# Attention and a SiLU layer on one core: new planner constants, an earlier V load, an earlier first product and another way of storing the last tiles

## The chip, the cores and the metric

The kernel runs on one core of one Trainium2 chip. The core has a matmul engine (TensorE, PE in the profile, with its weight loads as PEld), VectorE (DVE), ScalarE (ACT), GpSimd (POOL) and SyncE (SP). The metric is the device time of one execution in microseconds (us); lower is better. Transfers between HBM and the on-chip buffer are issued by POOL (all loads), SP and ACT (all stores).

## The reference

Inputs are q, k and v of 8 batches, 12 heads, 448 tokens and 64 values a head, and two weight matrices, 768 x 2048 (w_in) and 2048 x 768 (w_out), all float32. Per batch and head it computes softmax(q k^T / 8) v; the heads of a token are put side by side (3584 tokens x 768), and then comes

```python
h = x @ w_in
g = h * (1.0 / (1.0 + np.exp(-h)))
return (g @ w_out).astype(np.float32)
```

The output is 3584 x 768 float32.

## The kernel before, in words

**Work.** Everything is held in fp16 on chip; loads convert on the way. For a batch and a group of four heads (a unit; the first batch's units are cut in two halves of the tokens, so there are 27 units) the kernel transposes k and q on VectorE (lines 328, 338), computes scores in bursts of 8 or 16 matmuls into tiles `s` (line 357), takes exp on ScalarE into tiles `E` (line 394), and multiplies with ones (part 0, the sums) and with V (parts 1 and 2) into tiles `a` (lines 420, 436). VectorE turns the sums into reciprocals (`sT`, `inv`, `rdn`) and writes the scaled result to `xT` (line 493), already in the layout that the next product reads. V of the first batch lies in the buffer named `D` in the profile.

**First layer.** For batches 0 to 3, and for a part of batches 4 and 5, tiles `h` are x times w_in in groups of six matmuls (line 345). ScalarE takes tanh (line 521) and VectorE (1 + tanh) times h (line 559), which is the SiLU because x was halved. The other batches go in pairs: seven products on sums of halves in place of eight (tiles `f`, line 650, with copies and adds at 663 and 666), and SiLU on ScalarE (line 676). The results are in `G` and `X`.

**Second layer.** The first two tiles of 128 output tokens are plain products (tiles `o`, 16 matmuls for each half of the columns). All others go in quads, two token tiles by two column halves: seven products of eight matmuls each (tiles `p`, in the order 1, 5, 6, 2, 7, 3, 4, function `product`, queued by `queue_quad`). Products 1 and 2 share a bank: ScalarE must copy product 1 (line 768) before product 2 may add to it. Outputs leave by `take_out` (ScalarE copies the bank to a tile `ost`, line 771) or `add_out` (VectorE, line 780), and `store` issues four transfers of 32 rows for each (line 763), on SP, and for the last two quads on SP and ACT in turn.

**Order.** One stream of instructions per engine is written out by a planner in the kernel itself. The class `Order` holds for each engine the time when it is free, by constants at the head of the file: `SWITCH` for a change of the kind of tile on TensorE, `mm` and `act` for durations, `DMA_ROW`, `DMA_RATE`, `DMA_START`, `DMA_TAIL` for loads. At each step the main loop looks at the next score burst (`qk_at`), the next attention product (`av_at`) and a list `moe` of first- and second-layer work (`moe_ready`), and emits one that is ready by these times. Products are queued in parts of `PROD_AT` matmul positions; between two parts another piece of work may come in. `LATE` tells how long after the planned landing V of the first batch counts as there. Where the planner finds TensorE idle in the opening it fills with products of zeros (line 1530). Rings (`s_ring`, `m_ring`, `ost_ring` and others) stand for the buffers: two for scores, four banks for `h`, `a`, `o`, `p`, `f`, four for `ost`.

**Loads.** POOL issues all loads in one order, set by the calls of `plan_k`, `plan_q`, `plan_v`, `plan_w_in` and `plan_w_out`: k and q of the three head groups of the first batch, its V in four loads, three more q, half of w_in, and so on.

The readiness rule that the change touches is in `queue_quad`:

```python
elif m == 1 and qd > 1:
    made.append((pr_op.get((qd - 1, 6)), 9.0))
```

Product 1 of a quad may go only when product 6 of the quad before has been placed.

Of the kernel before, what the change touches and what calls it, by code (L numbers as in the profile page):

```python
# [13 lines left out]
ENG = mybir.EngineType  # L14


SWITCH = 0.094
PE_OUT = 0.20
HOP = 0.10
DMA_ROW = 0.022  # L20
DMA_RATE = 13570.0
DMA_START = 1.2
DMA_TAIL = 1.0

# [1 line left out]
def mm(n):  # L26
    return n / 2400.0 + 0.0026


def act(n):  # L30
    return n * 0.00087 + 0.13
# [47 lines left out]
class Order:  # L79
# [33 lines left out]
    def on_pe(self, op, mode):  # L113
        if mode == "full" and self.attention:
            mode, op.strips = "cols", True
        gap = SWITCH if mode != self.mode else 0.0
        self.mode = mode
# [3 lines left out]
    def load(self, rows, row_bytes, emit, ring=None, gate=None):  # L121
        op = Op("POOL", 0.58, emit)
        self.pool.append((op, rows * (DMA_ROW + row_bytes / DMA_RATE) / 16, ring, gate))
        return op
# [50 lines left out]
def kernel(  # L175
# [9 lines left out]
    nc = tc.nc  # L185

    B, NH, S, D = q.shape
# [3 lines left out]
    NG = NH // HG  # L191
    TPP = S // 32
# [9 lines left out]
    NT = 2 * S // 128  # L202
    OH = DM // 2
# [3 lines left out]
    NPL = 4  # L207
    EAGER = 1
    HALVES = 6
    NEAR, LATE = 0.15, -2.0  # L210
    COLD, FIRST = 8.5, 47
    SHY = 0.6
    TWB, SXB, FAR = 2, 2, 8
# [50 lines left out]
    rawk, rawq, KT, QT, E, T, acc, rdn_t, xT, g_t, ost_t = ({} for _ in range(11))  # L264
# [101 lines left out]
    def per_burst(n):  # L366
        return 2 if units[n][0] == 0 else 1
# [315 lines left out]
    S_t, tmp_t, ost_t, pr_t = {}, {}, {}, {}  # L683
# [57 lines left out]
    def bank(qd, m):  # L741
        return pr_t[(qd, m)][:, 0:OH]
# [5 lines left out]
    def ost(qd, i, j):  # L748
        t = sb.tile([128, OH], FP32, name=f"ost_{qd}_{i}{j}", tag="ost", bufs=NOST)
        ost_t[(qd, i, j)] = t  # L750
        return t

    def store(qd, i, j):
        u, t = divmod(2 * qd + i, NT)
        for w in range(4):
            r, col = divmod(128 * t + 32 * w, S)
            b = 2 * u + r
            dst = out[b * S : (b + 1) * S, OH * j : OH * (j + 1)].rearrange(
                "(i g) m -> g i m", g=TPP
            )  # L760

            eng = nc.scalar if w % 2 and 4 * qd + 8 >= NT * B else nc.sync
            eng.dma_start(  # L763
                out=dst[col // 32], in_=ost_t[(qd, i, j)][32 * w : 32 * (w + 1), :]
            )

    def take(qd, m):
        nc.scalar.copy(out=tmp(qd, m), in_=bank(qd, m))

    def take_out(qd, m, i, j):  # L770
        nc.scalar.copy(out=ost(qd, i, j), in_=bank(qd, m))  # L771
        store(qd, i, j)

    def add_in(qd, to, x, y):
# [25 lines left out]
    def plan_k(b, hg):  # L800
        ld_k[(b, hg)] = od.load(128, 2 * D * TPP, lambda: load_k(b, hg), rk_ring)

    def plan_q(n):
        g0, g1 = units[n][2:]
        ld_q[n] = od.load(128, 2 * D * (g1 - g0), lambda: load_q(n), rq_ring)

    def plan_v(b, hg0, hg1):
        made = []
        for x in range(4):
            ring = v_ring if (x == 0 and b > 0) else None  # L810
            heads, toks = HG * (hg1 - hg0), X_TOK[form(b, hg0)][x][1]
            made.append(
                od.load(32 * heads, 2 * D * toks, lambda x=x: load_v(b, hg0, hg1, x), ring)
            )
        for hg in range(hg0, hg1):
            ld_v[(b, hg)] = made
# [12 lines left out]

    NB0 = NG * len(PIECES)  # L830
    for hg in range(NG):
        plan_k(0, hg)
        plan_q(hg)
    plan_v(0, 0, NG)
    plan_q(NG)
    plan_q(NG + 1)
    plan_w_in(0, DFF // 2)
# [14 lines left out]
    for n in range(NB0 + NG, NU):  # L852
        b, hg = units[n][:2]
# [34 lines left out]
    pr_op, sg_op, w_op, plain_op = {}, {}, {1: [], 2: [], 3: []}, {}  # L888
    inv_op, norm_op = [], []
    quads, fourth, begun = [], [], []  # L890

    PROD_AT, FFN1_AT = 2, 2

    def in_parts(n, size, columns, emit, done, at=0):
        to = min(at + size, n)
# [311 lines left out]
    def queue_quad(qd):  # L1207
        quads.append(qd)
        fourth.append(qd)
        took = {}  # L1210

        def read(name, eng, fn, deps, then=None):
            busy = act(OH) if eng == "ACT" else OH / 960.0 + 0.13
            bias = -2 if eng == "ACT" else -4
            took[name] = od.add(Op(eng, busy, fn, deps, bias, then=then))

        def out(at):
            m_ring.give(at)
            ost_ring.give(at + STORE)

        def queue(m):
            def run():
                if BANK[m] == m:
                    m_ring.take()
                for ring, need in rings:
                    ring.take(need)
                in_parts(HF, PROD_AT, OH, lambda f0, f1: product(qd, m, f0, f1), done)

            def done(op):
                if m == 5:  # L1230
                    sg_ring.give(od.free["PE"] + PE_OUT)
                pr_op[(qd, m)] = op
                if m in (1, 5):
                    read(m, "ACT", lambda: take(qd, m), [op])
                elif m == 6:
                    read("u", "DVE", lambda: add_in(qd, 6, 6, 1), [op, took[1]], tmp_ring.give)
                    read("w", "DVE", lambda: add_in(qd, 5, 6, 5), [took["u"], took[5]])
                elif m == 2:
                    read("11", "ACT", lambda: take_out(qd, 1, 0, 0), [op], out)
                elif m == 7:  # L1240
                    read(
                        "22",
                        "DVE",
                        lambda: add_out(qd, 6, 5, 1, 1),
                        [op],
                        lambda at: (ost_ring.give(at + STORE), tmp_ring.give(at)),
                    )
                elif m == 3:
                    read("12", "ACT", lambda: take_out(qd, 5, 0, 1), [op], out)
                else:  # L1250
                    read("21", "ACT", lambda: take_out(qd, 6, 1, 0), [op], out)

            def deps():
                made = list(w_op.get(m, [None]))
                made += [took.get(x) for x in {2: (1,), 7: ("w",), 3: ("w",), 4: ("22",)}.get(m, ())]
                first = {5: 1, 6: 5, 7: 6, 3: 7, 4: 3}.get(m)
                if first:
                    made.append((pr_op.get((qd, first)), 9.0))
                elif m == 1 and qd > 1:
                    made.append((pr_op.get((qd - 1, 6)), 9.0))  # L1260
                if m in (1, 2, 4):
                    t = 2 * qd + (m == 4)
                    for b in {(128 * t + c) // S for c in (0, 127)}:
                        for f in range(HF):
                            x = g_op.get((b, f + HF * (m > 1)), [None])
                            made += [(y, f * mm(OH)) for y in x]
                    return made + ld_wout
                x = sg_op.get((qd, {5: 1, 6: 2, 7: 3, 3: 4}[m]), [])
                x = x if len(x) == 2 else [None, None]
                return made + [x[0], (x[1], 4 * mm(OH))]  # L1270

            rings = ((tmp_ring, 1),) if m in (1, 5) else ((ost_ring, 1),) * (m != 6)
            moe.append((deps, int(BANK[m] == m), run, rings))

        for m in (1, 5, 6, 2, 7, 3, 4):
            queue(m)
# [86 lines left out]
    def run_qk():  # L1363
        ns, c, ys = qk_seq.pop(0)
        n = ns[0]
        nq = 32 * (units[n][3] - units[n][2])
        s_ring.take(len(ys))
        if ys[0] == 0:
            e_ring.take()
        rest = len(ns) == 2  # L1370
        op = Op(
            "PE",
            2 * per_burst(n) * mm(nq) + (0.03 if rest else 0.013),
            (lambda: scores_rest(n)) if rest else (lambda: scores(n, c, ys)),
            tail=PE_OUT,
        )
        op.half = len(ys) == 1
        if c == NCH // per_burst(n) - 1 and ys[-1] == 1:
            done = []
            for m in ns:  # L1380
                if last_unit[units[m][:2]] == m:
                    done.append(kt_ring)
                done.append(rq_ring)
            op.then = lambda at: [r.give(at) for r in done]
        od.on_pe(op, "rest rows" if rest else "rows")
        for y in ys:
            made = od.add(
                Op(
                    "ACT",
                    act(2 * nq * per_burst(n)),  # L1390
                    lambda y=y: expo(n, c, y),
                    [op],
                    tail=0.2,
                    then=s_ring.give,
                )
            )
            for m in ns:
                exp_op.setdefault(m, []).append(made)
        if form(*units[n][:2]) != "lone" and c == 1 and ys[-1] == 1:
            adds.append(n)  # L1400
# [134 lines left out]
    while True:  # L1535
# [48 lines left out]
        if warm["on"] and od.free["PE"] <= od.now and wait > 0.06 and od.now > 0.9:  # L1584
            each = mm(128) if od.now > COLD else 0.107
            n = max(1, int((wait - 0.06) / each), int(wait / each + 0.9) * (od.now < COLD))
            if warm.pop("first", None):
                n = FIRST
# [36 lines left out]
```

## Time and profile before

| what | us |
|---|---|
| median of 3 runs | 393.24 (393.09 to 393.57) |
| the profiled execution's own time | 392.73 |
| its span, first to last instruction | 391.0 |
| TensorE busy | 383.1 |
| VectorE busy | 275.0 |
| ScalarE busy | 257.7 |
| granted TensorE clock, mean | 0.999 |

The span is what lies between the first and the last instruction in the profile; the rest of the execution's own time lies around it. Busy times are sums per engine, and an engine that is not on the chain of work that ended last may be idle at no cost. Times of events are counted from the start of the span.

### The profile page before, as it was taken

Reading aid. Unit: us, or ns where it says so; the run is one execution under the profiler, and the core shown is the slowest. Engines: PE = TensorE matmul, PEld = TensorE weight load, DVE = VectorE, ACT = ScalarE, POOL = GpSimd, SP = SyncE. Lnnn points to the kernel's source line nnn. Section 1 sums busy time; section 2 is a strip of 40 time slices with the busy share of each in tenths; the row PEclk is TensorE's granted clock in tenths of the full one; section 3 lists DMA queues with packets and bytes.
Section 4 is the critical chain, followed back from the end, with each engine's and each line's share of the span. In section 5 each row is a group of like instructions: output and inputs, shape, how many; then the busy total and the mean of one; then the engine's idle time right before and its main releaser. Section 6 shows DMA issues by size and latency. Waiting matters only on the chain.

```text
span 391.0 us, 13258 instructions
## 1 busy us (share of the span) xinstructions
PE 383.1 (98%) x5662; PEld 208.8 (53%) x5662; DVE 275.0 (70%) x571; ACT 257.7 (66%) x424; POOL 83.7 (21%) x153
## 2 busy tenths in 40 slices
PE   8999999999999999999999999999999999999995
PEld 6668764444445444455544454455546654555663
DVE  3476676999997858896878998599876235547322
ACT  4988885697967686966688776746763246763221
POOL 7532543604160422415060500000000000000000
PEclk9999999999999999999999999999999999999999
DMA  7999999834584672829492522210001330001343
GB/s 117 207 209 209 166 182 184 144 65 58 85 123 82 104 138 32 115 45 150 109 142 36 73 47 64 57 29 1 2 0 43 100 100 3 1 2 31 98 108 89
DMA packets 35594, 34.68 MB, mean 89 GB/s; under 512 B 11600, under 2 KB 34000, under 8 KB 35536
## 3 DMA queue, kind: packets, MB, share of 16 engines
q0 software_dynamic: 24784, 22.82, 39.0%
q1 hardware_dynamic: 9984, 10.24, 10.0%
q10 hardware_dynamic: 768, 0.79, 0.8%
q8 instruction: 44, 0.72, 0.8%
q14 instruction: 14, 0.11, 0.1%
HBM read 45.61 MB, written 11.01 MB: 145 GB/s over the span
## 4 chain that ended last, share of the span: by engine, by line
PE 94%; ACT 2%; DVE 2%; DMA 1%; issue 1%; ACTq 0%; DVEq 0%; POOLq 0%
PE p L345 30%; PE h L345 23%; PE s L357 13%; PE f L650 13%; PE a L420 11%; PE o L345 3%; PE a L436 2%; DMA rk<-in_k_dram 1%; ACT E L394 1%; DVE f L666 1%; PE z L1530 1%; ACTq L763 0%; DVE p L775 0%; ACT G L676 0%; ACT ost L771 0%
## 5 line engine op out<-in xcount | busy, mean ns | idle before, releaser
L394 ACT ACTIVATE E<-s 128x896 f16<-128x896 f32 (+1 forms) x172 | 151.2, 916 | 50.6 <-PE s L357 49.3
L345 PE MATMUL h<-xT,w_in_t 128*32 128x448 f16 (+2 forms) x1542 | 94.4, 342 | 0.0
L345 PEld LDWEIGHTS <-w_in_t 128*32 128x32 f16 (+1 forms) x1542 | 53.5, 97 | 38.2 <-issue 12.6
L345 PEld LDWEIGHTS <-G 128*32 128x32 f16 (+1 forms) x1184 | 52.6, 97 | 39.0 <-issue 8.4
L345 PE MATMUL p<-w_out_t,G 128*32 128x384 f16 (+1 forms) x872 | 66.2, 327 | 0.2
L293 POOL DMA_DIRECT2D V<-in_v_dram x84 | 46.0, 559 | 60.0 <-PE a L420 46.5
L357 PE MATMUL s<-rq,KT 32*128 32x448 f16 (+4 forms) x864 | 56.9, 340 | 1.2 <-ACT E L394 0.8
L559 DVE SCALAR_TENSOR_TENSOR G<-th,h 128x448 f16<-128x448 f16 (+2 forms) x92 | 44.3, 498 | 13.2 <-ACT th L521 13.1
L521 ACT ACTIVATE th<-h 128x448 f16<-128x448 f32 (+1 forms) x92 | 42.2, 485 | 16.8 <-PE h L345 9.8
L771 ACT COPY ost<-p 128x384 f32<-128x384 f32 x39 | 18.7, 481 | 33.2 <-PE p L345 24.1
L345 PE MATMUL p<-D,S 128*32 128x384 f16 (+1 forms) x496 | 37.4, 327 | 0.0
L420 PE MATMUL a<-E,V 128*32 128x448 f16 (+1 forms) x672 | 36.3, 353 | 0.0
L493 DVE SCALAR_TENSOR_TENSOR xT<-a,rdn 128x448 f16<-128x448 f32 (+1 forms) x54 | 30.1, 568 | 8.3 <-PE a L420 6.4
L357 PEld LDWEIGHTS <-KT 32*128 32x128 f16 (+2 forms) x864 | 17.6, 98 | 29.6 <-issue 27.2
L676 ACT ACTIVATE G<-f 128x448 f16<-128x448 f32 (+1 forms) x52 | 25.9, 529 | 10.6 <-PE f L650 6.8
L279 POOL DMA_DIRECT2D rq<-in_q_dram x27 | 15.0, 556 | 73.5 <-PE s L357 51.6
L345 PEld LDWEIGHTS <-S 128*32 128x32 f16 (+1 forms) x496 | 20.6, 97 | 14.5 <-issue 2.3
L666 DVE TENSOR_TENSOR f<-f,q 128x448 f32<-128x448 f32 x26 | 16.4, 632 | 15.6 <-PE f L650 14.2
L405 DVE TENSOR_TENSOR T<-T,E 128x1792 f16<-128x1792 f16 x20 | 21.7, 1085 | 7.8 <-ACT E L394 7.8
L420 PEld LDWEIGHTS <-V 128*32 128x32 f16 (+1 forms) x672 | 17.1, 96 | 16.4 <-issue 5.8
L405 DVE TENSOR_TENSOR T<-E,E 128x1792 f16<-128x1792 f16 x20 | 21.7, 1084 | 4.4 <-ACT E L394 4.3
L650 PEld LDWEIGHTS <-w_in_t 128*128 128x128 f16 x156 | 15.3, 98 | 14.1
(135 smaller groups left out, 384.8 us busy)
## 6 DMA issues: line engine op xcount, KB each, us to landing
out_dram<-ost SPq DMA_DIRECT2D x208, 48.0 KB, 1.6
rk<-in_k_dram POOLq DMA_DIRECT2D x24, 224.0 KB, 5.2
rq<-in_q_dram POOLq DMA_DIRECT2D x21, 224.0 KB, 4.9
w_in_t<-in_moe_w_in_dram POOLq DMA_DIRECT2D x6, 512.0 KB, 11.2
w_out_t<-in_moe_w_out_dram POOLq DMA_DIRECT2D x4, 768.0 KB, 13.2
V<-in_v_dram POOLq DMA_DIRECT2D x43, 64.0 KB, 4.0
V<-in_v_dram POOLq DMA_DIRECT2D x40, 48.0 KB, 3.7
out_dram<-ost ACTq DMA_DIRECT2D x16, 48.0 KB, 1.8
```

The source lines that it names most:

```text
L293: nc.gpsimd.dma_start(out=v_of(b, hg0)[32 * x : 32 * (x + 1), at, 0:count, :], in_=v[b, hs].rearrange("h (i g) d -> i h g d", g=TPP)[:, :, ...
L345: nc.tensor.matmul(out=out[at], lhsT=lhsT[:, at], rhs=rhs, **flags)
L357: nc.tensor.matmul(out=pS[p0 : p0 + 32 * (x1 - x0), h % 2, at : at + nq], lhsT=KT[(b, hg)][32 * h : 32 * (h + 1), c, x0:x1, :, e], rhs=QT[ ...
L394: nc.scalar.activation(out=E[(n, w)][0:kr, 2 * y : 2 * y + 2, 0:nk], in_=pS_t[(n, w, y)][0:kr, :, 0:nk], func=AF.Exp, scale=attn_scale,)
L405: nc.vector.tensor_tensor(out=T[n], in0=T[n] if step else E[(n, 0)], in1=E[(n, step + 1)], op=ALU.add,)
L420: nc.tensor.matmul(out=a[32 * h : 32 * (h + 1), 0:nq], lhsT=w, rhs=e[k0:k1, h, at : at + nq], start=start, stop=stop,)
L493: nc.vector.scalar_tensor_tensor(out=x3(b, cc)[:, cc % 3, 32 * g0 : 32 * g1], in0=acc[(n, part)][:, 0:nq], scalar=0.5, in1=rdn_t[n].rearra ...
L521: nc.scalar.activation(out=th, in_=h_t[(b, f, t0)][:, 0 : t1 - t0], func=AF.Tanh)
L559: nc.vector.scalar_tensor_tensor(out=dst[:, f, at + lo : at + hi], in0=th_t[(b, f, t0)][:, lo - t0 : hi - t0], scalar=1.0, in1=h_t[(b, f, ...
L650: nc.tensor.matmul(out=pp_t[(f, PBANK[m])], lhsT=w[:, c, :], rhs=a[:, c, :], start=(c == 0 and m in (1, 6, 5)), stop=(c == 2), skip_group_ ...
L666: nc.vector.tensor_tensor(out=pp_t[(f, to)], in0=pp_t[(f, x)], in1=pf_t[(f, y)], op=ALU.add)
L676: nc.scalar.activation(out=dst[:, f, at + lo : at + hi], in_=pp_t[(f % HF, x)][:, lo:hi], func=AF.Silu, scale=2.0,)
```

## The change

Six things are changed together. The planner's constants for a change of tile kind, for loads, for score bursts and for exps have new values, and V of the first batch counts as there 1 us after its planned landing, not 2. V of the first batch is loaded after the third k and before the third q (the loop value 2 meets the second condition). Products of the second layer are queued matmul position by position, so a score burst may come between any two. Product 1 of a quad may go once product 1 of the quad before is placed. In the last quad the copy of the last product is VectorE's. And the four outputs of the last quad are stored by two transfers of 64 rows each, one from SP and one from ACT, in place of four of 32 rows.

```diff
-SWITCH = 0.094
+SWITCH = 0.104
 PE_OUT = 0.20
 HOP = 0.10
-DMA_ROW = 0.022
-DMA_RATE = 13570.0
+DMA_ROW = 0.012
+DMA_RATE = 14000.0
...
-    NEAR, LATE = 0.15, -2.0
+    NEAR, LATE = 0.15, -1.0
...
     def store(qd, i, j):
         u, t = divmod(2 * qd + i, NT)
+        if qd == NT * B // 4 - 1:
+            r, col = divmod(128 * t, S)
+            g, b = col // 32, 2 * u + r
+            dst = out[b * S : (b + 1) * S, OH * j : OH * (j + 1)].rearrange(
+                "(i g) m -> g i m", g=TPP
+            )
+            for w in range(2):
+                (nc.scalar if w else nc.sync).dma_start(
+                    out=dst[g + 2 * w : g + 2 * w + 2],
+                    in_=ost_t[(qd, i, j)][64 * w : 64 * (w + 1), :],
+                )
+            return
         for w in range(4):
...
     def take_out(qd, m, i, j):
-        nc.scalar.copy(out=ost(qd, i, j), in_=bank(qd, m))
+        if m == 6 and qd == NT * B // 4 - 1:
+            nc.vector.tensor_copy(out=ost(qd, i, j), in_=bank(qd, m))
+        else:
+            nc.scalar.copy(out=ost(qd, i, j), in_=bank(qd, m))
         store(qd, i, j)
...
     for hg in range(NG):
+        if hg == 2.5:
+            plan_v(0, 0, NG)
         plan_k(0, hg)
+        if hg + 0.5 == 2.5:
+            plan_v(0, 0, NG)
         plan_q(hg)
-    plan_v(0, 0, NG)
     plan_q(NG)
...
-    PROD_AT, FFN1_AT = 2, 2
+    PROD_AT, FFN1_AT = 1, 2
...
-                    read("21", "ACT", lambda: take_out(qd, 6, 1, 0), [op], out)
+                    eng = "DVE" if qd == NT * B // 4 - 1 else "ACT"
+                    read("21", eng, lambda: take_out(qd, 6, 1, 0), [op], out)
...
                 elif m == 1 and qd > 1:
-                    made.append((pr_op.get((qd - 1, 6)), 9.0))
+                    made.append((pr_op.get((qd - 1, 1)), 9.0))
...
-            2 * per_burst(n) * mm(nq) + (0.03 if rest else 0.013),
+            2 * per_burst(n) * mm(nq) + (0.041 if rest else 0.024),
...
-                    act(2 * nq * per_burst(n)),
+                    act(2 * nq * per_burst(n)) - 0.07,
                     lambda y=y: expo(n, c, y),
                     [op],
-                    tail=0.2,
+                    tail=0.27,
```

## The prediction

> **What bounds the kernel now.** I read the page's busy shares first, then the chain of work that ended last, then the timeline of TensorE (PE) for places where it pauses, and last the stores.
>
> ```profile
> span 391.0 us, 13258 instructions
> ...
> PE 383.1 (98%) x5662; PEld 208.8 (53%) x5662; DVE 275.0 (70%) x571; ACT 257.7 (66%) x424; POOL 83.7 (21%) x153
> ...
> q1 hardware_dynamic: 9984, 10.24, 10.0%
> q10 hardware_dynamic: 768, 0.79, 0.8%
> ...
> PE 94%; ACT 2%; DVE 2%; DMA 1%; issue 1%; ACTq 0%; DVEq 0%; POOLq 0%
> ...
> out_dram<-ost SPq DMA_DIRECT2D x208, 48.0 KB, 1.6
> ```
>
> PE is busy 98% and makes 94% of the chain: only a pause of PE, or work before its first and after its last product, can move the end. The timeline shows where these are (start, length, engine, line; idle time before it and what ended it in brackets):
>
> ```profile
> 12.88 0.57 PE L357 MATMUL s<-rq,KT 32*128 32x224 f16 x8
> ...
> 15.87 0.57 PE L420 MATMUL a<-E,D 128*32 128x224 f16 x16
> ...
> 60.27 0.55 POOL L279 DMA_DIRECT2D rq<-in_q_dram  x1 [3.67 <-DMA w_out_t<-in_moe_w_out_dram]
> ...
> 103.34 1.47 PE L345 MATMUL p<-w_out_t,G 128*32 128x384 f16 x32
> 104.74 0.60 PE L357 MATMUL s<-rq,KT 32*64 32x448 f16 x16
> 105.39 0.83 PE L345 MATMUL p<-w_out_t,G 128*32 128x384 f16 x16
> ...
> 166.11 1.48 PE L345 MATMUL p<-w_out_t,X 128*32 128x384 f16 x32 [0.61 <-ACT 1_3_4110 L768]
> ...
> 287.89 0.73 PE L650 MATMUL f<-xT,tw 128*128 128x448 f16 x3 [0.23 <-DVE f L666]
> ...
> 385.30 1.46 PE L345 MATMUL p<-D,G 128*128 128x384 f16 x8
> ...
> 387.24 0.48 ACT L771 COPY ost<-p 128x384 f32<-128x384 f32 x1 [0.99 <-DMA out_dram<-ost]
> 387.75 0.85 ACTq L763 DMA_DIRECT2D out_dram<-ost  x2
> ```
>
> Groups of matmuls that follow without a wait overlap by 0.16 in this record (1.46 shown for 1.30 of advance), so a pause is 0.16 more than the idle shown: 0.61 at 166.11 is 0.77. The last lines are the tail: the last product ends at 386.77, the last copy starts only at 387.24, since ACT was still issuing stores, and its four stores land until 389.97 by the landing marks; the span ends 1.03 later.
>
> The sum stands against this execution: span 391.0, its own time 392.73 (1.73 around the span). The median of the runs, 393.24, is 0.51 above it, and I add that at the end. 0.2% of it, 0.79 us, is about what a measurement of this kernel can tell from no change.
>
> **Part by part.**
>
> *Refitted constants, PROD_AT.* They change only the order. In the two built orders the same products stand (18 fills with zeros fewer), and PE changes its kind of tile between equally many stretches, 193 in each without the fills. A change costs 0.105 (a 448-column product's start to a score's start is 0.294 instead of 0.189). Equal counts: 0.
>
> *V ahead of the third q.* On POOL's queue the third q load is issued after four V loads (4 x 0.63), at 6.5 instead of 4.03. By the landing marks q landed at 10.38 and the last V at 14.42; the same bytes are ahead of whichever is last, so V lands at 13.6 to 14.2 and q at 13.8 to 14.4. PE now has the first product with V ahead of the third unit's scores. Counting by rows (0.50 a burst of scores or a product with its change), it reaches that product at 12.4 and waits 1.2 to 1.8; the scores start at 14.3 to 14.85 instead of 12.88. After that, 18 zero fills fewer (0.06 each and a change of kind) stand in the order and three first-layer groups (0.58 each) come earlier; at 32 us it is ahead by 0.2 to 0.75. Then it gives that back: the plain product of the first two output tiles takes its last quarter of w_out at 58.9 instead of 63.6, and the fourth w_out load landed at 59.7 (POOL's q load, held by it, starts at 60.27). It waits about 0.8, and from there the rows bring both orders to the same place near 75 us. All loads behind keep their places. Sum to 75: 0, bounds -0.3 and +0.3.
>
> *The first product early.* It may follow the previous quad's first product, so the copy (0.48 on ACT, behind exps of 0.92) has time before product 2 reads what it left. Where 0.75 and 0 us lay between products 1 and 2 (lines at 104.74 and 166.11), 4.5 to 5.1 lie in the new order; both waits go: -0.12 and -0.77. What is late next: the bank that product 1 holds longer; the shortest reuse distances of the four banks stay as they were (1.0 before, 0.9 after).
>
> *The pair stage, 269 to 293.* Four waits of 0.16, 0.39, 0.39 and 0.22 end by silu or add. One product moves under the third: 1.30 of cover instead of 1.13, -0.17. The waits at 323, 351 and 382 have the same neighbours and stay.
>
> *Waits that I can't see.* Before, 0.29 of small waits are left between 75 and 269. The new order is planned with an ACT 0.07 an exp faster and scores often 2.7 apart instead of 2.9. I take +0.3; bounds -0.3 and +1.2.
>
> PE's end: -0.12 - 0.77 - 0.17 + 0.3 = -0.76.
>
> *The last copy on VectorE.* No such copy is in the trace; nearest is the add on the same tile, 0.558 (L780), bounds 0.48 (ACT's copy) and 0.60. DVE is free, starts 0.03 after the product's end, at 386.81 instead of 387.24: ends 0.35 earlier.
>
> *64-row stores.* Eight instead of sixteen in the last quad, one issue less on each of SP's and ACT's queues: the last issue starts at once, not 0.42 later. A pattern of three dimensions may take longer to issue: between the 0.31 of these stores and the 0.72 of POOL's loads. Against that stands how a store is spread. 9984 packets for 208 stores are 48 each: 32 rows and 16 marks of 4 bytes, so a store of 32 by 384 lies on 16 engines, two rows on each. The new stores have 64 rows on the SBUF side but 2 x 32 on the other. No transfer of the trace from SP or ACT has such a count, so I bound it. One end: 16 engines, four rows each, two rows more at 0.09 (10.0% of 16 x 391 over 6656 rows) is +0.2; with copy and issue the tail is 0.6 shorter. Other end: the split runs along the outermost count and must fall in the same places on both sides. 64 and 2 then allow two pieces of 32 rows on two engines. Since both queues used the same 16 engines, all eight stores then fall on the same two: 4 x 64 = 256 rows each. A row takes 0.059 at the rate of the opening's k loads (8 rows of 3584 B an engine in 1.1 us) to 0.0895 (the mean packet above). I take 0.065, near the first, because a long queue resembles those loads. First issue 383.15 - 0.76, first packet 0.81 later (as the last stores show), + 16.6, mark to landing 0.36, to the end 1.03: 401.2, which is +10.2. DVE's early copy is buried under it, and PE isn't held: no output buffer of that quad is used again.
>
> Between these far ends I take the second: equal pieces of whole rows on each side is what all stores shown have, and with 2 there are only two.
>
> [...]
>
> Sum: 392.73 + 10.2 = 402.9; with the 0.51 of the median 403.4.
>
> **Rivals.**
>
> 1. *The stores spread over 16 engines* (not slower). Then -0.76 - 0.6: 392.73 - 1.4 + 0.51 = 391.9, bounds 390.9 and 393.1. For it: every store so far has 16 marks. Against: none has an outer count under 32. It decides at the split: over eight engines (32 rows each in all, about 2 us at 0.065, mostly beside the remaining products) it would still be no slower.
> 2. *Two engines a store, but others for each queue*: 128 rows, 8.3 us: 383.2 + 8.3 + 0.36 + 1.03 = 392.9, time 395.1. With a new pair for each store, 32 rows of 2.1 us behind the last copy end at 390.9: 393.1, no change. Against: both queues show the same 16 engines' marks.
> 3. *The early part takes the gain too*: the fourth w_out load lands 1 us later (they took 4.3, 3.6, 5.3, 4.2), or exps end late at the bursts 2.7 apart (0.1 at each of 30). Either takes rival 1's time to 393, within 0.2%.
> 4. *The freed waits come back* as a wait for a bank held by two first products: 0.9 more, 392.8 in rival 1.
>
> **How the numbers follow.** The same two engines: 0.55. Rival 1 as it stands 0.26, with rivals 3 or 4 in it 0.06 more. Rival 2: 0.13. The likeliest gives 403.4, its own range 401.5 (0.059 a row) to 409.7 (0.0895). Since 0.32 lies near 392, the range reaches down to rival 1: 391.0 to 408.5, which leaves out the slowest rows and rival 1's best edge. Faster: 0.26 less its part above 392.45, 0.24. Same: 0.10 from rivals 1, 3, 4 and the last of 2. Slower: 0.55 + 0.11, 0.66.
>
> **What the new profile would show.** The two hardware queues' last stores with long issue-to-landing times, several to 15 us, and DMA share near 2/16 with PE idle from 386: right. All landing within 2.2 us and the span under 390: rival 1. PE's last product should end near 386.0; no wait before any second product at 105 and 166; a wait before the w_out product near 59 us; a wait of 1.2 to 1.8 before the first product with V. The forecast falls with the split of the stores alone; if PE's end isn't 0 to 1.5 earlier, my reading of the order is wrong.

## The result, and the profile after

The changed kernel takes 411.76 us (median of 5, 411.05 to 413.04) against 393.11 of the kernel before on the same chip: 1.0472 times as long, 95% interval 1.045 to 1.0495. The forecast was 403.4, so the sign was right and the size 8.4 short. Against the span worked out there for the profiled execution, 401.2, it is 411.3.

The page after, in the order of the lines shown of before:

```profile
span 411.3 us, 13177 instructions
...
PE 390.2 (95%) x5626; PEld 211.2 (51%) x5626; DVE 276.2 (67%) x572; ACT 257.0 (63%) x423; POOL 83.6 (20%) x153
...
PEclk9856999999999999999999999999999999999995
...
q1 hardware_dynamic: 9864, 10.24, 9.5%
...
q10 hardware_dynamic: 648, 0.79, 0.7%
...
PE 89%; DMA 2%; DVE 2%; ACT 1%; POOL 1%; issue 1%; DVEq 0%; ACTq 0%; POOLq 0%
...
out_dram<-ost SPq DMA_DIRECT2D x200, 48.0 KB
```

PE is busy 7.1 us longer (390.2 against 383.1) although its real work is the same. The row `PEclk` is the granted clock in tenths of full speed, in 40 slices of the span; in the page of before it held only 9s:

```profile
PEclk9999999999999999999999999999999999999999
```

Now it has 8, 5 and 6 in its second to fourth slice, and a 5 in the last, where PE has nothing left to do. The packets of the two hardware queues give away how the new stores are split: 9864 is 200 stores of 48 and four of 66, 648 is eight of 48 and four of 66. A 64-row store is 64 rows and 2 marks, where a 32-row store was 32 rows and 16 marks.

The opening, in stretches of 3.41 us: in the traces of this case the time from one change of the recorded clock to the next is a multiple of 3.413 us (here 20.48 at half clock, 361.81 at full clock behind it). The columns are from, to and length; PE busy and its instructions; granted clock; DMA share; GB/s:

```profile
6.89:10.30 3.41, 2.96 (x44) 1.00 1.23 179
10.30:13.72 3.42, 3.04 (x63) 1.00 1.43 196
13.72:17.13 3.41, 1.60 (x41) 1.00 1.16 210
17.13:20.54 3.41, 3.41 (x53) 0.50 1.12 211
...
34.20:37.61 3.41, 3.41 (x46) 0.50 1.15 209
37.61:41.02 3.41, 3.33 (x88) 1.00 1.17 213
```

In one stretch PE was busy 1.60 of 3.41 us. At its end the clock falls to half, and it stays there for 20.5 us, six stretches, although PE is busy in all of them. The timeline shows what PE waited for:

```profile
13.37 0.57 PE L420 MATMUL a<-E,D 128*32 128x224 f16 x16 [0.38 <-DMA D<-in_v_dram]
...
15.28 0.78 DVE L338 STREAM_TRANSPOSE rq<-rq 128x224 f32<-128x224 f32 x2 [2.57 <-DMA rq<-in_q_dram]
...
15.75 0.57 PE L357 MATMUL s<-rq,KT 32*128 32x224 f16 x8 [1.81 <-DVE rq L338]
```

V was there at 13.33, earlier than forecast; the third q landed only at 15.26, behind it, and PE's next scores started when its transpose was done, at 15.75. The last product ended at 394.87 instead of 386.77.

The second loss follows that product. The copy on VectorE starts at 394.91, ends at 395.47, and its stores are issued 0.03 later. Then the core only waits for its stores (all engines; here PE, PEld, DVE, ACT, POOL busy, clock, DMA share of 16 engines, GB/s):

```profile
393.00:395.00 2.00, 1.87 (x12) 0.91 (x10) 0.09 (x1) 0.48 (x1) 0.00 (x0) 1.00 0.12 28
395.00:397.00 2.00, 0.00 (x0) 0.00 (x0) 0.47 (x1) 0.00 (x0) 0.00 (x0) 1.00 0.13 41
...
400.00:405.00 5.00, 0.00 (x0) 0.00 (x0) 0.00 (x0) 0.00 (x0) 0.00 (x0) 0.50 0.13 50
405.00:409.00 4.00, 0.00 (x0) 0.00 (x0) 0.00 (x0) 0.00 (x0) 0.00 (x0) 0.50 0.13 50
409.00:410.00 1.00, 0.00 (x0) 0.00 (x0) 0.00 (x0) 0.00 (x0) 0.00 (x0) 0.50 0.10 38
```

The last 4 us of the kernel before, whose last product ended at 386.77, in the same columns:

```profile
387.00:391.00 4.00, 0.00 (x0) 0.00 (x0) 0.00 (x0) 0.48 (x1) 0.00 (x0) 0.90 0.41 98
```

A share of 0.13 is two engines of sixteen, though both queues have stores waiting: they share the same two. From the last product's end to the span's end it is 16.4 us instead of 4.2.

So 20.3 us more span are 8.1 in PE's end and 12.2 behind it. Two of 68 executions of the kernel before were slow, with a mean clock of 0.956 and 0.953 (407.8 and 409.4 us), and so was one of four with the 128-row stores below (415.7 us, 0.948); these are left out of the ratios.

### The profile page after: what moved, and what is told of

The parts are those of the page before. It is cut to its first block, busy times and chain, and to the rows that moved or that the text cites. A ratio compares the mean times of both kernels' runs of the same rounds, so it can differ in the third digit from the quotient of the medians.

```text
span 411.3 us, 13177 instructions
## 1 busy us (share of the span) xinstructions
PE 390.2 (95%) x5626; PEld 211.2 (51%) x5626; DVE 276.2 (67%) x572; ACT 257.0 (63%) x423; POOL 83.6 (20%) x153
## 3 DMA queue, kind: packets, MB, share of 16 engines
q1 hardware_dynamic: 9864, 10.24, 9.5%
## 4 chain that ended last, share of the span: by engine, by line
PE 89%; DMA 2%; DVE 2%; ACT 1%; POOL 1%; issue 1%; DVEq 0%; ACTq 0%; POOLq 0%
PE p L345 28%; PE h L345 22%; PE f L650 12%; PE s L357 12%; PE a L420 11%; PE o L345 3%; DMA rq<-in_q_dram 2%; PE a L436 1%; ACT E L394 1%; DVE f L666 1%; POOL D L293 1%; POOL rk L273 0%; DVE p L790 0%; DVE T L405 0%; POOL rq L279 0%
## 5 line engine op out<-in xcount | busy, mean ns | idle before, releaser
L345 PE MATMUL h<-xT,w_in_t 128*32 128x448 f16 (+2 forms) x1524 | 96.5, 343 | 0.2 <-DVE G L559 0.2
L357 PE MATMUL s<-rq,KT 32*128 32x448 f16 (+4 forms) x864 | 60.3, 357 | 2.6 <-DVE rq L338 1.8
L493 DVE SCALAR_TENSOR_TENSOR xT<-a,rdn 128x448 f16<-128x448 f32 (+1 forms) x54 | 30.4, 569 | 11.9 <-PE a L420 10.1
L357 PEld LDWEIGHTS <-KT 32*128 32x128 f16 (+2 forms) x864 | 19.3, 105 | 33.6 <-issue 29.8
L345 PEld LDWEIGHTS <-S 128*32 128x32 f16 (+1 forms) x496 | 20.5, 97 | 14.9 <-issue 3.1
```

Source lines behind the costliest of these rows:

```text
L345: nc.tensor.matmul(out=out[at], lhsT=lhsT[:, at], rhs=rhs, **flags)
L357: nc.tensor.matmul(out=pS[p0 : p0 + 32 * (x1 - x0), h % 2, at : at + nq], lhsT=KT[(b, hg)][32 * h : 32 * (h + 1), c, x0:x1, :, e], rhs=QT[ ...
L493: nc.vector.scalar_tensor_tensor(out=x3(b, cc)[:, cc % 3, 32 * g0 : 32 * g1], in0=acc[(n, part)][:, 0:nq], scalar=0.5, in1=rdn_t[n].rearra ...
```

## The experiments

In most of them the part under test is the opening, so the mean clock of single executions is given: with 32-row stores 0.996 to 1.000 is a kept clock (what is missing lies behind the last product).

**The changed kernel with 32-row stores.** The branch of `store` for the last quad is taken out. The second run is the same kernel once more, to see how far the throttled stretch repeats.

```diff
     def store(qd, i, j):
         u, t = divmod(2 * qd + i, NT)
-        if qd == NT * B // 4 - 1:
-            ...
-            return
         for w in range(4):
```

> The changed kernel with its last quad stored in 32-row stores again (all else stays: V early, refitted constants, PROD_AT 1, last copy on VectorE). My theory is that two separate things cost the time: TensorE's clock, granted at 0.50 from 17 to 37 us, puts its last product at 394.9 instead of 386.8; and the 64-row stores add some 12 us behind that product. Then the last product still ends at 394 to 395, the mean clock stays at 0.96, and the span ends 3.9 behind it: about 400 us by the clock, 398 to 401 with the spread of the throttled time. If instead the late last product had to do with the stores (their issues stand in the queues of SP and ACT ahead of the last copies), the last product comes earlier than 392 and the time is below 396.

> A second copy of the previous kernel with one look, to see how far its last product and the length of the throttled stretch repeat: theory 394 to 395 and 17 to 20.5 us at 0.50.

Median 400.56 (397.53 to 403.36, four executions; mean clock 0.962 to 0.983), 1.0184 times before with a wide interval (1.0116 to 1.0251), and 401.4 (0.966) for the second. The share of the stores is gone, the other loss is there and even larger than I expected: the last product ends at 397.6 and at 395.6, and the half clock lasts nine and eight stretches. And the place was not the one that I expected. First the one, then the other run, in the same columns as above:

```profile
6.26:9.67 3.41, 1.80 (x34) 1.00 1.10 163
9.67:13.09 3.42, 3.42 (x31) 0.50 1.47 193
...
40.39:43.81 3.42, 3.33 (x88) 1.00 1.16 212
```

```profile
4.46:7.87 3.41, 2.48 (x49) 1.00 1.08 160
7.87:11.29 3.42, 2.87 (x50) 1.00 1.27 168
11.29:14.70 3.41, 3.41 (x51) 0.50 1.36 200
```

Here the clock fell at 9.67 and at 11.29, before PE came to the wait for the third q at all. In the first, q's first load landed at 6.96, where it had been 5.41 in the first profile of the changed kernel, and PE waited 1.26 us for it (1.18 in this stretch); in the second the stretch had only 0.55 us of waits. So the wait of 1.81 for the third q is one way to lose the clock, not the only one: three traces of this opening lost it in three places, and q's first load alone came 1.55 us later in one of them than in another.

**The kernel before with 64-row stores alone, and with 128-row stores.** The first adds the same branch of `store` to the kernel before; the second issues one store for each of the last four tiles:

```diff
+        if qd == NT * B // 4 - 1:
+            ...
+            (nc.scalar if j else nc.sync).dma_start(
+                out=dst[g : g + 4], in_=ost_t[(qd, i, j)][:, :]
+            )
+            return
```

> The kernel before with the 64-row stores alone (last copy still on ACT). If these stores lie on two engines, their first is issued at 383.15 and the span ends 20.0 later, as in the changed kernel (411.3 - 391.26): 403.2, and 1.73 around it gives 404.9. With the row time that I had forecast, 0.065, it would be 403.7. If the long tail of the changed kernel were a consequence of its lower clock or of its order, the time would be within 2 us of the 393.1 of before.

> The kernel before with one 128-row store for each of the last four output tiles (first and third on SP, others on ACT): the side of the output has 4 pieces of 32 rows. If the number of engines follows the outermost count, each store lies on 4 engines and they take 128 rows each: DMA share 4/16, first issue 383.15 + 0.81 + 128 rows at 0.069 + 0.36 + 1.03 = 394.2, time 395.9. If it were always two engines for a store with such a count: 404 to 405, as with the 64-row stores. If it were 16: no slower than 393.5. In all of these the last product stays at 386.8.

64 rows: 405.88 (405.85 to 406.08), 12.5 over the 393.40 of before and 1.0 over my number; in the profile the last product comes 1.02 later than in that of before, the first store is issued at 384.17, and the span ends 19.9 later (20.0 in the changed kernel). 128 rows: 399.97 (three executions; 1.017, interval 1.0148 to 1.0192). Its tail:

```profile
388.00:391.00 3.00, 0.00 (x0) 0.00 (x0) 0.00 (x0) 0.00 (x0) 0.00 (x0) 1.00 0.25 66
391.00:395.00 4.00, 0.00 (x0) 0.00 (x0) 0.00 (x0) 0.00 (x0) 0.00 (x0) 0.52 0.25 85
395.00:396.00 1.00, 0.00 (x0) 0.00 (x0) 0.00 (x0) 0.00 (x0) 0.00 (x0) 0.50 0.08 31
```

A share of 0.25 is four engines, for a store whose output side has 4 pieces; with 2 pieces it was two. The number of engines follows the outermost count, in the two cases tried. The time was 3 to 4 over my estimate for four engines, since the rows were slower: 128 on each engine took about 11 us, 0.086 a row instead of 0.069. Why is not shown.

**The changed kernel with more fills.** 32-row stores, and more matmuls with zeros ahead of certain bursts of scores; in the second kernel 20 more ahead of the first product with V:

```diff
+    EXTRA = {(0, 0, 0): 8, (0, 1, 0): 6, (1, 0, 0): 8, (2, 0, 0): 28}
...
-            (lambda: scores_rest(n)) if rest else (lambda: scores(n, c, ys)),
+            (lambda: scores_rest(n)) if rest else (lambda: (run_zeros(EXTRA.get((n, c, ys[0]), 0)), scores(n, c, ys))),
...
-            lambda: attend(ns, part),
+            lambda: (run_zeros(20 if (ns[-1], part) == (0, 1) else 0), attend(ns, part)),
```

> The changed kernel with 32-row stores and 50 more fills with zeros in the opening (8 and 6 ahead of the first unit's second-stream-free bursts, 8 ahead of its third burst, 28 ahead of the third unit's scores, where TensorE waited 1.81 us). Theory: the clock is withdrawn after any stretch of 3.413 us in which the matmuls cover less of the array than about 0.36 (rows x columns x moving columns over 128 x 128 x 8192; the traces so far: withdrawn after 0.193, 0.307 and 0.353, kept from 0.379 up). The fills add 0.016 each, so every stretch of the opening is over 0.4: no withdrawal, the last product at 386 to 387, time 391.5 to 393.5. Rival: the order itself costs the 8 us (early V, first-layer groups before their time) and the low clock only goes with it: then 398 or more whatever the fills do.

> As the kernel with 50 more fills, and 20 more ahead of the first product with V, where its profiled execution waited 1.71 us for V without a fill and lost the clock at once (15.27 us). Theory: with both waits filled the clock is kept in every execution, so the times lie between 392.6 and 394.0 (the full-clock executions of the other were 392.67 to 393.58, and 20 fills of 0.056 can cost up to 1.1 where nothing is waited for). Rival: the clock is lost for another reason than the idle time, then again some four in nine executions lie between 395 and 400.

The first: five of nine executions kept the clock (392.67 to 393.58, mean 0.999 to 1.000), but four lost it for a short time (395.5 to 400.2, mean 0.983 to 0.995), where I had expected none. Its profiled execution is one of the four:

```profile
8.44:11.85 3.41, 3.41 (x59) 1.00 1.41 186
11.85:15.27 3.42, 1.71 (x35) 1.00 1.30 204
15.27:18.68 3.41, 3.41 (x42) 0.50 1.12 211
18.68:22.09 3.41, 3.41 (x71) 1.00 1.14 210
...
28.92:32.33 3.41, 2.18 (x64) 1.00 1.09 198
32.33:35.75 3.42, 3.42 (x54) 0.50 1.12 204
```

V landed late in it, and PE stood 1.71 us in front of the first product with V, where no fill is. With 20 fills there as well, all eleven executions kept the clock: 393.50, 392.88 to 394.93, four of them over the 394.0 that I had given as the top. So the loss of some 7 us (400.56 against 393.50) is the clock, and fills in the waits keep it. The rival, that the order itself costs those us, is excluded: it is the same order with fills added.

**The kernel before with smaller fills, and with none.** Its 40 fills behind the first 47 use 32 columns of the array instead of 128, or are left out. First the edit for the smaller fills, then the one for none:

```diff
+            m = 128 if n == FIRST else 32
             nc.tensor.matmul(
-                out=warm["z"][:, 0:128], lhsT=zeros, rhs=zeros, start=True, stop=True
+                out=warm["z"][0:m, 0:128], lhsT=zeros[:, 0:m], rhs=zeros, start=True, stop=True
             )
```

```diff
-        for _ in range(n):
+        for _ in range(n if n == FIRST else 0):
```

> The kernel before, with its 40 fills behind the first 47 cut to 32 columns of the array (same count, places and moving columns, so TensorE is as busy as before). If the clock goes by how long TensorE is idle, nothing changes: 393.1. If it goes by the share of the array that the matmuls cover, the stretches of the opening that held 9 and 19 fills fall from 0.42 and 0.48 to about 0.31 and 0.25, the clock is withdrawn by 8 to 15 us and not given back before the first layer's products at about 38 us: 400 to 409 us.

> The kernel before without its 40 fills behind the first 47; the order of all real work is the same. If idle time in a stretch of 3.413 us decides, the stretches that held 9 and 19 fills get 0.6 to 1.5 us of idle time more, near or over the 1.6 that has always cost the clock: most executions lose it and take 397 to 409, and the profile shows 0.50 from 11 to 15 us on. If fills do not matter: 393.1, clock 1.0.

Smaller: 393.02, ten executions of 392.88 to 393.79, all with the clock kept; ratio 0.9995 (0.9986 to 1.0004). None: 405.04 (404.25 to 405.22), clock lost in all four, ratio 1.0291 (1.0275 to 1.0308). The profiles, first the smaller fills, then none:

```profile
8.41:11.82 3.41, 3.41 (x58) 1.00 1.36 186
11.82:15.24 3.42, 3.42 (x53) 1.00 1.35 202
```

```profile
5.03:8.44 3.41, 1.95 (x37) 1.00 1.03 158
8.44:11.85 3.41, 3.29 (x46) 0.50 1.39 190
...
42.57:45.98 3.41, 3.41 (x76) 1.00 1.25 177
```

My theory, that the clock is withdrawn below a fixed share of the array, fell: a fill of a quarter of the columns keeps it as well. For the fills of this kernel it is enough that PE is busy; whether idle time alone decides is another question, and the last section comes back to it. And the fills are worth some 12 us in the kernel before, with not one instruction of real work changed.

**One half of the opening's edits at a time.** All three with 32-row stores: the kernel before with V early; the changed kernel with V late; the changed kernel with V early and only the two DMA constants of before.

```diff
         plan_k(0, hg)
+        if hg == 2:
+            plan_v(0, 0, NG)
         plan_q(hg)
-    plan_v(0, 0, NG)
```

> The kernel before with only V's first four loads ahead of the third q load; the constants of before stay, with which the order has 20 fills ahead of the third unit's scores instead of 4. My step says 0 (-0.3 to +0.3) as long as the clock is kept, and by the theory it is kept, since the wait is filled: 392.8 to 393.6. If the early V itself makes the loss, 398 or more.

> The changed kernel with 32-row stores and V's loads behind the third q again; the refitted constants stay, and with them the order has 4 fills ahead of the third unit's scores and 70 in all. If V ahead of q alone makes the long wait, the clock is kept and the time is 391.5 to 393. If the refitted constants (fewer fills) are enough, the clock is lost in most executions: 396 to 404.

> The changed kernel with 32-row stores, V early, and only the two DMA constants of before (0.022 a row, 13570 a us): the order then has 22 fills ahead of the first product with V, 93 in all. If the loss comes from waits that the refitted DMA constants no longer foresee, the clock is kept at least through 17 us in most executions and the time is 392 to 395; if V early loses the clock whatever the fills, 398 to 404.

V late in the changed kernel: eight of ten executions lost the clock (396.4 to 402.75), the two others took 391.25 and 391.34. In the profiled one PE stood in front of the first product with V without a fill (total, times, longest):

```profile
PE a L420 <- DMA D<-in_v_dram: 1.4, 1, 1.4
```

V early is not needed to lose the clock, then. The early first product and the copy are no cause either, since the kernel before with these two (below) kept it in all six executions; what is left are the planner's refitted constants. V early with the old DMA constants, whose order has 22 fills in front of the first product with V: one of ten lost it (401.89), median 393.05. The planner places fills where it foresees a wait; told that loads land earlier, it foresees shorter waits than there are. With V early the traces have 20 and 22 fills in a row in front of the long wait under the old DMA constants, and a single one under the new.

V early in the kernel before missed the time that I held likelier, 392.8 to 393.6, and came out at the other: 398.69 (398.43 to 399.22), ratio 1.0141 (1.0127 to 1.0155), with the clock kept (mean 0.996 to 0.999). This loss is not in the opening. Its list of PE's waits:

```profile
PE s L357 <- ACT E L394: 1.9, 4, 0.8
PE f L650 <- DVE f L666: 1.5, 1, 1.5
...
PE f L650 <- DVE xT L493: 0.8, 2, 0.5
PE a L436 <- ACT E L394: 0.4, 1, 0.4
```

Most of these lie between 264 and 296 us. There the order differs from that of before: the last scores start at 267.2 instead of 254.2 and the last attention products at 272.3 instead of 263.8, while the last tiles `h` of the first layer start at 263.9 instead of 269.5, so that none of this work is left to cover the waits. In the first 26 us of the pair stage 18 matmuls of the second layer stand instead of 31. PE's idle time is 6.8 instead of 2.6 us; that is 4.2 of the 5.6 us of span. PE also pauses 22 times instead of 10; if each costs 0.16 more than the idle time shown, as the prediction worked out, that is an estimated 1.9 and could be the rest. An edit of 4 loads changes the order 260 us later.

**The first product and the copy alone.** The kernel before with `PROD_AT = 1`, its rule in `queue_quad` and the copy on VectorE.

> The kernel before with only two of the edits: PROD_AT 1 with its rule (the first product of the next output tiles may follow the previous quad's first) and the last copy on VectorE. Constants, V's place, 32-row stores are those of before. My steps give -0.12 and -0.77 for the waits at 105 and 166 and -0.35 for the copy: 1.2 below before, 392.0 against 393.2. Rival: the freed waits come back as waits for a bank or a scratch tile: within 0.4 of before.

392.05 (391.91 to 392.31), 0.997 of before (0.9958 to 0.9982): 1.2 was expected and 1.3 measured against the median of before, 393.37. The waits at 105 and 166 are gone from its profile. That the sum fits so well is in part luck, since the copy brought less than its 0.35 (next section).

**The order with the clock kept.** The changed kernel with V late, 32-row stores and 24 fills ahead of the first product with V; a second with 12 more; and the changed kernel as it is, with its 64-row stores and the 70 fills.

> V's loads behind the third q, refitted constants, PROD_AT 1, last copy on VectorE, 32-row stores, and 24 more fills ahead of the first product with V, where the profiled execution without them waited 1.4 us and lost the clock. If the clock is kept, the order's own gain shows: the two full-clock executions without these fills took 391.3, 24 fills are 1.34 us in a place where TensorE waits 1.4, so 391.2 to 392.2 in nearly every execution. If the order brings nothing but my -0.35 for the copy: 392.7 to 393.2.

> As the kernel before it, with 12 more fills (6, 2 and 4 ahead of the first three bursts), which should keep the clock in an execution whose first q or k loads land late. Same times, 391.3 to 392.5, with fewer slow ones; up to 0.6 more if the opening has no room for the fills.

> The changed kernel with its 64-row stores and 70 more fills, so that the clock is kept. If the two losses add up, what is left is the stores: the 393.5 of the same kernel with 32-row stores plus the 12.5 that the 64-row stores added to the kernel before, 406.0. If the stores' loss depends on the clock or the order: more than 1.5 off that.

The first: 391.51 (391.33 to 391.71), 0.9955 of before (0.9942 to 0.9968); the second 391.43 (391.18 to 392.26), 0.9958. Neither lost the clock in an execution. Both beat both kernels. What PE waits for in the first:

```profile
PE z L1534 <- DVE zeros L230: 1.0, 1, 1.0
PE s L357 <- ACT E L394: 0.6, 2, 0.4
PE f L650 <- ACT X L676: 0.3, 1, 0.3
PE h L345 <- DVE G L559: 0.2, 1, 0.2
PE f L650 <- ACT G L676: 0.2, 1, 0.2
```

Its last product ends at 385.73, 1.04 before that of the kernel before, in the two profiles. The changed kernel with 70 fills takes 406.17 (405.83 to 406.38): 393.50 with 32-row stores and the 12.5 of the 64-row stores are 406.0. So the stores cost the same in this order as in that of before, and 5.6 of the changed kernel's 411.76 are left for the clock, within the 4.0 to 9.9 by which the four executions with 32-row stores and no added fills lie above 393.50.

## Why the prediction was right or wrong

- **64-row stores**: right in mechanism. Two engines for each store, the same two for both queues. A store has 66 packets (64 rows and 2 marks), and the share is 0.13 with the stores of both queues waiting; the 128-row stores, with 4 pieces on the output side, had a share of 0.25, four engines. That the split must fall in the same places on both sides was a supposition of mine: the runs show, for 2 and 4, that the engines were as many as the output's pieces, although the SBUF side has 64 and 128 rows. The term was mis-sized a little: from the first store's issue the span ends after 20.0, and the terms summed to 18.8. The rows ran from 392.1 to 409.8, 256 on each engine, 0.069 each instead of 0.065: 0.061 once 50 GB/s flow (25 an engine, 1536 bytes a row), up to 0.11 at the 28 GB/s between 393 and 395. Rivals 1 and 2 are out. (The low end of this case's own range, 401.5, should have been 401.9 by its rows: 256 of 0.059.)
- **V ahead of the third q, "sum to 75: 0"**: this step failed, and with it PE's end. I had the size of the wait about right (1.2 to 1.8 forecast; 0.38 in front of V and 1.81 in front of q measured) and its place wrong: it fell to q, which landed at 15.26 instead of 14.4 at the latest, behind V. What the step had wrong is the price of such a wait. I had counted that 18 fills fewer stand in the order, and booked that as time gained, 0.06 each; but the fills were what kept the clock, and V early kept it in all four and in nine of ten executions where 20 or 22 fills stood in front of the wait. PE's end was forecast at 386.01 and came at 394.87: 8.9 of the 10.1 by which the span missed, the other 1.2 being mostly the stores' rows. Nor did the wait of 0.8 for the fourth w_out load come, which was to take back the opening's gain: with V early, 70 fills and the clock kept, no pause of PE between 20 and 270 us is longer than 0.18.
- **The clock, for which the prediction has no term.** In all five executions of the changed kernel it was lost: their mean is 0.961 to 0.965, where 0.982 to 0.985 is a kept clock with these long stores (the changed kernel with 70 fills). The step on V took it that a wait of 1.8 us costs its own length and nothing else. No run had shown that, and it does not hold: with 1.81 us of idle time in one stretch of 3.41 the clock fell to 0.50 and stayed there for 20.48 us, and in other runs 1.23 to 1.71 us in a stretch, once 0.55, went ahead of the half clock.
- **Constants, "equal counts: 0"**: wrong for the same reason. The number of changes of tile kind is about equal (183 and 186 recorded), but the DMA constants decide where fills stand. The run with the new constants and V late lost the clock in eight of ten executions, and with 24 fills at its wait in none of five.
- **First product early**: right. No wait is left at 105 and 166 in any kernel that has it, and with the copy it is worth 1.3; rival 4, a wait for a bank in their place, did not come.
- **Pair stage, -0.17, and unseen waits, +0.3**: both too cautious. Before, the idle times shown there are 0.23, 0.23 and 0.06; in the changed kernel and in the best one about 0.26 and 0.06, and behind the opening no new wait above 0.2 us came up elsewhere. PE's end with the clock kept and V late is 1.04 earlier; I had -0.76.
- **V early with the clock kept**: not settled. With 70 fills PE ends 2.0 behind the kernel with V late and 24, but 45 fills more are 2.5 us of PE time themselves, and how many of these lie in waits can't be told apart. The kernel with V early and the old DMA constants has 46 fills behind the first 47, nearly as many as the 47 of the one with V late and 24, and its last product ends 1.9 later too; but it also has another order.
- **Last copy on VectorE**: it takes 0.558, as estimated, and starts 0.04 after the product's end; it and the stores' issues come 0.35 earlier, as forecast. But from the last product to the span's end it is 4.00 in the kernel with V late and 24 fills against 4.19 before, so 0.19 are gained instead of 0.35; the stores take longer to land. I haven't traced why.

## What to carry to other kernels

Look at matmuls on zeros that keep TensorE busy in a wait as part of the timing and not as waste (without its 40 fills the kernel before took 405.04 us, with them 393.23): before moving loads or refitting a planner's load times, list the waits that the new order leaves uncovered, and look at the granted clock over the first 50 us. Before merging stores, look at the outermost count on both sides: 64 rows in 2 pieces went through two DMA engines, and eight stores of 96 KB took 17.7 us where those of 48 KB had each landed within 1.8 us of their issue. An opening that loses the clock in some executions shows in the spread of single executions before it shows in their median: with 50 fills the median was 393.58, and four of nine executions took 395.5 to 400.2.

## What the hardware showed that I had not expected

- *Losing the clock.* In the traces of these kernels the clock was withdrawn in the opening after stretches with 1.81 us of PE idle time out of 3.41 (the changed kernel), 1.71 and 1.23 (50 fills), 1.61 (32-row stores), 1.46 (no fills) and 1.4 (V late), and once with 0.55 (32-row stores, second run); it was kept in all others there, with up to 1.0 (0.97 with the quarter-size fills). Outside the opening it was kept through a wait of 1.46 (the kernel before with V early, 295 us), and around the last product, where full-array matmuls run until PE stops, after a stretch with 1.13 (the changed kernel, 392.6 to 396.0). So idle time alone doesn't decide. The share of the array that the matmuls cover sorts the stretches of the opening better. I count it as rows x columns x moving columns over 128 x 128 x 8192, a fixed divisor: matmuls of 384 columns start 0.163 us apart at full clock, so about 8,000 columns fit in a stretch. It was 0.19 to 0.34 where the clock was withdrawn, 0.37 and more where it was kept. But three stretches with the quarter-size fills kept it at 0.26, 0.32 and 0.34, two of them without idle time. What the chip measures stays open; nothing here explains both.
- *Getting it back.* Without added fills PE was busy at half clock through five to ten stretches, nearly all of them without a gap, before it got the clock back: at 37.6 us in the changed kernel, where six matmuls of the first layer stand in the stretch before, and at 38.6, 40.4 and 42.6 in three other runs. With the 28 fills it came back after one stretch, at 18.68. The 20.5 us at half clock are why 2 us of waits cost 8. In the changed kernel the covered share, now over half that divisor, was 0.51 to 0.69 in the five stretches behind which the half clock went on, and 0.73 in the sixth, behind which full clock came back. That the covered share is the cause is read from these stretches and was not tried by itself.
